# Attention and two mixtures of experts on one core: wide reciprocals, two first pairs taken together, and the decoding of the fourth weight block put behind the last ordered pair

## The chip, the cores and the metric

The kernel runs on one core of one Trainium2 chip. The metric is the device time of one execution in microseconds; the times given are medians of several runs. An engine's name is PE (TensorE), DVE (VectorE), ACT (ScalarE), POOL (GpSimd) or SP (SyncE, which only issues transfers here).

## What is computed

Attention over 4 batches, 12 heads, 448 positions and 64 numbers per head, with queries and keys normalised by their root mean square; then a dense feed-forward layer on the 1792 tokens of 768 numbers; then a layer in which a gate sends each token to one of 8 experts. The reference, cut:

```python
def _attn_ref(q, k, v, g_q, g_k):
    def rmsnorm(x, g):
        rms = np.sqrt(np.mean(x * x, axis=-1, keepdims=True) + 1e-06)
        return x / rms * g
    q_n, k_n = (rmsnorm(q, g_q), rmsnorm(k, g_k))
    scale = 1.0 / np.sqrt(q.shape[-1])
    scores = scale * np.matmul(q_n, k_n.transpose(0, 1, 3, 2))
    scores = scores - np.max(scores, axis=-1, keepdims=True)
    attn = np.exp(scores)
    attn = attn / (np.sum(attn, axis=-1, keepdims=True) + 1e-09)
    return np.matmul(attn, v).astype(np.float32)

def _moe_ref(x, w_in, w_out):          # x 1792x768, w_in 768x2048, w_out 2048x768
    h = x @ w_in
    g = np.maximum(0.01 * h, h)
    return (g @ w_out).astype(np.float32)

def _moe2_ref(x, w_gate, w_output_gate, w1, w2):   # 8 experts, 768 to 1024 to 768
    ...
    for e in range(E):
        mask = e_idx == e
        ...
        h = np.maximum(x[mask] @ w1[e], 0.0)
        ye = h @ w2[e]
        out[mask] = gate_w[mask, None] * eom[mask, e, None] * ye
    return out.astype(np.float32)
```

## The kernel before

**Attention** goes over 24 pairs: a batch and two heads that share the 128 partitions. The 448 positions are cut into 4 chunks (`NC`) of 112 rows (`CP`). For one pair:

- `load` fetches queries and keys (`qk`) and values (`vv`); `square` squares on ACT (`sq`) and sums on DVE (`ms`); `roots` makes the reciprocal roots by nine small DVE steps on all pairs that `together` put side by side; `norm` multiplies (`qn`) on POOL, and for the first pair one half of it on DVE.
- `turn_k` and `turn_q` transpose `qn` on PE (bank `tr`) and split the result in a high and a low part (`kh`, `qh` on ACT, `kl`, `ql` on DVE), of which three products make up one.
- `top` makes the scores of one chunk a first time in a bank `tp`, whose maxima DVE takes (`md`); `row` transposes the four maxima (`tr`, then `mx` on ACT).
- `probs` makes the scores of a chunk with all parts and less the maximum (`sc`, four matmul lines); ACT takes their exp (`p`, for chunk 0 `pr`). `values` multiplies them with `vv` into `av`. POOL adds the four `p` up in `pr`.
- `sums` and `back` bring the sums of the exps, by PE (`tr`, ACT `sp`, then `av`), to DVE, which takes the reciprocal `r`, 112x8. `spread` brings `r` to the layout of `av` (`tr`), `scale` copies that on ACT (`rt`) and multiplies `av` on DVE, and `store` splits the result into `xTh` (ACT) and `xTl` (DVE), the input of the next layer.

The bank `tp` and the bank of `sc` exist once, `tr` twice (`TRB`). So a `top` waits for the `md` of the one before, and `probs` for the exp of the one before.

Pairs 0 to 2 are written out in `begin`, pairs 3 to 22 in `steady` (`prev` is the pair before, `one`, `two` and so on those behind `cur`). There the order of PE, DVE, ACT and POOL is that of the code (`manual_schedule`). The last pair goes by `ORDER`, and a scheduler sets units of the first feed-forward layer in its gaps.

**Weights.** The feed-forward weights lie in memory as 64-bit numbers. `Weights.decode` turns half a block, 128x384 numbers, into 32-bit ones: one transfer into `wd` (one buffer), `mag` on ACT, `top` twice, a compare, `pw` and `raw` on DVE, an add into `raw` on POOL. `RAW` is 3, the number of blocks that can wait in `raw`; `split` turns a block to its high and low part (ACT, POOL). Six halves are decoded within pairs 8 and later (`work(i)`), every second pair one. The halves after these are decoded in `advance`, which the scheduler places; the matmuls of the first layer (`first`, `second`: `mo`, `mp`) take their weights from there.

Of the kernel before, what the change touches and what calls it, by code (L numbers as in the profile page):

```python
# [20 lines left out]
def attention_moe_moe2(  # L21
# [40 lines left out]
    def lo_of(engine, dst, src, hi):  # L62
        engine.tensor_tensor(dst, src, hi.bitcast(F32), ALU.subtract)  # L63
# [91 lines left out]
    class Attention:  # L155
# [30 lines left out]
        def square(self, st):  # L186

            n = 4 * NC
            flat = st["qk"].rearrange("p t h (c d) -> p (t h c) d", d=DH)
            sq = self.early.tile([CP, n, DH], F32, name="sq", bufs=2)  # L190
            for h in (slice(0, n // 2), slice(n // 2, n)) if st is self.first else (slice(0, n),):
                nc.scalar.activation(sq[:, h], flat[:, h], AF.Square, scale=DH ** -0.5)
                nc.vector.tensor_reduce(st["ms"][:, h], sq[:, h], AX.X, ALU.add)
# [68 lines left out]
        def turn_k(self, st, i):  # L262
# [5 lines left out]
            nc.vector.scalar_tensor_tensor(kl, tk, gg, kh.bitcast(F32), ALU.mult, ALU.subtract)  # L268
            st.update(kh=kh, kl=kl)

        def top(self, st, c):

            sc = self.tp()
# [78 lines left out]
        def store(self, st):  # L352
# [3 lines left out]
            lo_of(nc.vector, xl, t, xh)  # L356

        def pieces(self):
# [35 lines left out]
            for op in ORDER:  # L394
                if op == "S":
                    self.sums(sts[n - 2])
                    self.back(sts[n - 2])
                elif op == "C":
# [7 lines left out]
            self.back(last)  # L406
            yield
# [5 lines left out]
        def begin(self, i, sts):  # L413

            cur, one, prev = sts[i], sts[i + 1], sts[i - 1] if i else None
            if i == 0:
                todo = [[("square", 2)], [("roots", 2, 3), ("norm", 2)], [("square", 3)],
                        [("square", 4), ("roots", 3, 5)]]
            elif i == 1:
                todo = [[("norm", 3)], [("square", 5)], [("norm", 4)], []]  # L420
            else:
                todo = [[("square", 6)], [("roots", 5, 7), ("norm", 5)], [("norm", 6)], []]
            for lo, hi in {0: ((2, 3), (3, 5)), 1: ((5, 7),)}.get(i, ()):
                self.together(sts[lo:hi])
            for c in range(NC):
                if c == 3 and prev:
                    self.scale(prev)
                self.probs(cur, c)
                if i == 0 and c == 0:
                    self.turn_k(one, 1)  # L430
                    self.turn_q(one, 1)
                self.top(one, c)
                if c == 2 and prev:
                    self.back(prev)
                if c:
# [5 lines left out]
                elif c == 2 and prev:  # L441
                    self.spread(prev)
# [13 lines left out]
        def steady(self, i, sts):  # L456
# [46 lines left out]
            self.back(prev)  # L503
            self.values(cur, 1)
            self.spread(prev)
# [5 lines left out]
            if at(i + 6):  # L511
                self.square(at(i + 6))
            yield

            self.scale(prev)
            self.probs(cur, 3)
            if two:
                self.top(two, 0)
            self.values(cur, 2)
            self.store(prev)  # L520
            self.row(one)
# [14 lines left out]
    class Weights:  # L536
# [26 lines left out]
        def decode(self, parts=2):  # L563

            n = D // 2
            for _ in range(parts):
# [13 lines left out]
                nc.scalar.activation(mag, hi.bitcast(F32), AF.Abs)  # L580
                nc.vector.tensor_scalar(top, hi, 3, 0x3FFFFFF8, ALU.logical_shift_left, ALU.bitwise_and)
# [530 lines left out]
```

## Time and profile before

| | |
|---|---|
| median of 3 runs | 1232.29 us (1229.84 to 1232.62) |
| profiled execution | 1230.19 us, span of its trace 1228.4 us |
| PE busy | 1158.2 us, 94% of the span |
| DVE busy | 775.5 us, 63% |
| ACT busy | 500.3 us, 41% |
| POOL busy | 456.4 us, 37% |

The shares are averages over parts of the program with different limits; attention ends at some 365 us, and everything that the change touches lies before 420 us. In the trace, a time in square brackets is how long the engine was idle ahead of an instruction, and what it then waited for. PE's records of the same line in a row are put into one row with their count.

### The profile page before, as it was taken

The numbers are of one execution on the slowest core, as the hardware profiler recorded it, in microseconds if no ns is written. First come the engines' busy times: TensorE is split into PE (matmuls) and PEld (weight loads), VectorE is DVE, ScalarE is ACT, GpSimd is POOL, SyncE is SP. The second block draws the span as 40 slices with busy tenths as digits, with TensorE's granted clock in tenths as the row PEclk, the third lists the DMA queues.
The fourth block names the chain that finished last, engine by engine and source line by source line (L and its number), as shares of the span: only waits on it lengthen the run. The fifth ranks groups of instructions, "written<-read, shape, count | busy, mean of one in ns | idle before, by whom it ended". The sixth has DMA issues, their size and how long they took to land.

```text
span 1228.4 us, 19094 instructions
## 1 busy us (share of the span) xinstructions
PE 1158.2 (94%) x6988; PEld 930.8 (76%) x6988; DVE 775.5 (63%) x1326; ACT 500.3 (41%) x791; POOL 456.4 (37%) x301
## 2 busy tenths in 40 slices
PE   4899999989899899999999999999799999999997
PEld 2455555545568788888888889888598988998986
DVE  6777888876627786858585854446745179215446
ACT  2566666655335422222222321132344167225444
POOL 1667767757324331313232220000414047113334
PEclk9999999989899999999999999999699999999999
DMA  5212222111102220202020200343357059413456
GB/s 149 60 47 61 68 80 73 50 29 29 46 13 77 78 77 26 78 26 78 26 78 26 78 26 1 133 118 88 117 199 249 24 197 354 153 47 125 172 201 227
DMA packets 68081, 116.28 MB, mean 95 GB/s; under 512 B 6780, under 2 KB 45948, under 8 KB 67968
## 3 DMA queue, kind: packets, MB, share of 16 engines
q1 hardware_dynamic: 64528, 103.87, 26.6%
q0 software_dynamic: 3120, 11.02, 2.6%
q8 instruction: 57, 0.93, 0.3%
q14 instruction: 56, 0.46, 0.1%
q10 hardware_dynamic: 320, 0.00, 0.0%
HBM read 106.61 MB, written 12.58 MB: 97 GB/s over the span
## 4 chain that ended last, share of the span: by engine, by line
PE 77%; DVE 10%; issue 5%; ACT 3%; DMA 2%; POOL 2%; ACTq 0%; DVEq 0%; POOLq 0%; SPq 0%
PE mo L627 6%; PE mo L628 6%; PE mo L629 6%; PE sc L298 6%; PE av L309 6%; PE mp L646 6%; PE mp L647 5%; PE mp L648 5%; PE ph L990 4%; PE ph L989 3%; PE ph L988 3%; PE py L1006 3%; PE py L1004 3%; PE py L1005 3%; DVE w1l L63 2%
## 5 line engine op out<-in xcount | busy, mean ns | idle before, releaser
L654 DVE TENSOR_TENSOR ysum<-mp,ysum 128x448 f32<-128x448 f32 x168 | 103.8, 621 | 111.1 <-PE mp L648 109.5
L313 POOL TENSOR_TENSOR pr<-pr,p 112x896 f32<-112x896 f32 x72 | 153.2, 2128 | 49.6 <-ACT p L300 35.4
L627 PE MATMUL mo<-xTh,w0h 128*128 128x448 f32 x384 | 142.8, 372 | 13.2 <-DVE g L634 9.4
L646 PE MATMUL mp<-gh,w1h 128*128 128x448 f32 x384 | 144.4, 377 | 1.4 <-ACT ysum L652 0.7
L628 PE MATMUL mo<-xTl,w0h 128*128 128x448 f32 x384 | 141.8, 369 | 0.2 <-DVE xTl L63 0.2
L647 PE MATMUL mp<-gl,w1h 128*128 128x448 f32 x384 | 141.8, 369 | 0.0
L629 PE MATMUL mo<-xTh,w0l 128*128 128x448 f32 x384 | 141.4, 368 | 0.0
L648 PE MATMUL mp<-gh,w1l 128*128 128x448 f32 x384 | 140.4, 368 | 0.0
L588 POOL TENSOR_TENSOR raw<-raw,top 128x384 f32<-128x384 f32 x64 | 65.2, 1020 | 191.1 <-DVE raw L586 166.7
L277 DVE TENSOR_REDUCE md<-tp 112x2 f32<-112x896 f32 x96 | 104.4, 1088 | 17.7 <-PE tp L275 17.4
L1004 PE MATMUL py<-w2h,hT 128*128 128x384 f32 x288 | 99.7, 346 | 0.0
L63 POOL TENSOR_TENSOR w1l<-r,w1h 128x1024 fp32r<-128x1024 f32 x17 | 42.9, 2528 | 149.4 <-ACT w1h L952 75.1
L1006 PE MATMUL py<-w2l,hT 128*128 128x384 f32 x288 | 96.8, 336 | 0.0
L1005 PE MATMUL py<-w2h,hL 128*128 128x384 f32 x288 | 96.5, 335 | 0.0
L63 DVE TENSOR_TENSOR hL<-pt,hT 128x512 fp32r<-128x512 f32 x36 | 24.8, 689 | 106.3 <-ACTq L1014 59.3
L627 PEld LDWEIGHTS mo<-xTh,w0h 128*128 128x128 f32 x384 | 72.5, 189 | 24.1 <-DVE g L634 12.1
L990 PE MATMUL ph<-w1l,xgh 128*128 128x512 f32 x216 | 86.4, 400 | 4.2 <-DVE w1l L63 4.2
L988 PE MATMUL ph<-w1h,xgh 128*128 128x512 f32 x216 | 86.7, 402 | 0.0
L989 PE MATMUL ph<-w1h,xgl 128*128 128x512 f32 x216 | 85.8, 397 | 0.0
L63 POOL TENSOR_TENSOR w1l<-raw,w1h 128x768 fp32r<-128x768 f32 x16 | 31.4, 1984 | 141.7 <-ACT w1h L596 141.7
L646 PEld LDWEIGHTS mp<-gh,w1h 128*128 128x128 f32 x384 | 72.4, 189 | 13.0 <-DVE ysum L654 4.1
L300 ACT ACTIVATE p<-sc 112x896 f32<-112x896 f32 x72 | 66.0, 917 | 39.8 <-PE sc L298 35.6
(199 smaller groups left out, 2499.8 us busy)
## 6 DMA issues: line engine op xcount, KB each, us to landing
r<-in_moe_w_dram SPq DMA_DIRECT2D x27, 1024.0 KB, 5.5
r<-in_moe_w_dram SPq DMA_DIRECT2D x36, 768.0 KB, 7.3
wd<-in_moe_w_in_dram SPq DMA_DIRECT2D x32, 384.0 KB, 3.3
wd<-in_moe_w_out_dram SPq DMA_DIRECT2D x32, 384.0 KB, 3.1
qk<-in_q_dram SPq DMA_DIRECT2D x24, 224.0 KB, 3.0
qk<-in_k_dram SPq DMA_DIRECT2D x24, 224.0 KB, 3.2
vv<-in_v_dram SPq DMA_DIRECT2D x24, 224.0 KB, 2.8
x2d<-xn SPq DMA_DIRECT2D x24, 224.0 KB, 2.9
```

What stands on the lines that cost most here:

```text
L63: engine.tensor_tensor(dst, src, hi.bitcast(F32), ALU.subtract)
L313: nc.gpsimd.tensor_tensor(st["pr"][:CP], st["pr"][:CP], p, ALU.add)
L627: nc.tensor.matmul(ph, wh_[:, c], xh, start=(c == 0), stop=False)
L628: nc.tensor.matmul(ph, wh_[:, c], xl, start=False, stop=False)
L629: nc.tensor.matmul(ph, wl_[:, c], xh, start=False, stop=(c == KD - 1))
L646: nc.tensor.matmul(py, hi[:, sl], gh, start=(j == 0), stop=False)
L647: nc.tensor.matmul(py, hi[:, sl], gl, start=False, stop=False)
L648: nc.tensor.matmul(py, lo[:, sl], gh, start=False, stop=(j == GF - 1))
L990: nc.tensor.matmul(ph[n], xh[:, c], w1l[:, c, s_], start=False, stop=(c == K1 - 1))
L1004: nc.tensor.matmul(py[n], hT[:, c], w2h[:, c, s_], start=(c == 0), stop=False)
L1005: nc.tensor.matmul(py[n], hL[:, c], w2h[:, c, s_], start=False, stop=False)
L1006: nc.tensor.matmul(py[n], hT[:, c], w2l[:, c, s_], start=False, stop=(c == K2 - 1))
```

## The change

Four things. `spread` no longer multiplies each of the eight columns of `r` by the identity, but transposes a copy `wide` (112x512) of `r`, each number 64 times, which ACT makes (`widen`); in `steady` it moves from behind `values(cur, 1)` to behind `row(one)`, and `scale` behind `values(cur, 2)`. At the start, the first two pairs' squares and roots are taken together, both transposes of pair 1 stand among the tops of pair 0, and these tops use the `sc` bank for every second chunk. In `begin`, pair 2 has its roots alone, and pairs 3 and 4 theirs one pair later. And the `mag` and the first `top` of the fourth block (`k == RAW`) are issued after the store seen last (`issue_after`). The diff, cut:

```diff
@@ constants
+    def join_constants():
         nc.vector.scalar_tensor_tensor(gg, gg, ROOT ** -2, gk, ALU.mult, ALU.mult)
@@ norm
-                (nc.vector if t and st is self.first else nc.gpsimd).tensor_tensor(
+                (nc.vector if st is self.first else nc.gpsimd).tensor_tensor(
@@ top
-        def top(self, st, c):
-            sc = self.tp()
+        def top(self, st, c, other=0):
+            sc = self.sc() if other else self.tp()
@@ widen, spread
+        def widen(self, st):
+            wide = self.pool.tile([CP, NC, 2, DH], F32, name="wide", bufs=1)
+            nc.scalar.activation(
+                wide, st["r"].rearrange("p j c -> p c j").unsqueeze(3).to_broadcast([CP, NC, 2, DH]), AF.Copy)
+            st["wide"] = wide
+
         def spread(self, st):
-            tr = st["tr"] = self.tr()
-            for c in range(NC):
-                for j in range(2):
-                    nc.tensor.matmul(
-                        tr[j * DH:(j + 1) * DH, c * CP:(c + 1) * CP],
-                        st["r"][:, j, c:c + 1].to_broadcast([CP, DH]), ident[:CP, :CP], start=True, stop=True)
+            st["tr"] = self.turned_of(st["wide"].rearrange("p c j d -> p c (j d)"))
@@ the start
-                st = sts[0]
-                self.together(sts[:1])
+                st, one = sts[:2]
+                self.together(sts[:2])
                 self.square(st)
-                self.roots(sts[:1])
-                self.norm(st)
+                self.square(one)
+                join_constants()
+                self.roots(sts[:2])
+                self.norm(st, (1, 0))
+                self.norm(one, (1, 0))
                 self.turn_k(st, 0)
                 self.turn_q(st, 0)
-                self.together(sts[1:2])
                 for c in range(NC):
-                    self.top(st, c)
+                    self.top(st, c, c % 2)
                     if c == 1:
-                        self.square(sts[1])
-                self.roots(sts[1:2])
+                        self.turn_k(one, 1, apart=True)
+                        self.turn_q(one, 1, apart=True)
                 self.row(st)
-                self.norm(sts[1])
+                one["klow"]()
+                one["low"]()
...
@@ begin
-                        [("square", 4), ("roots", 3, 5)]]
+                        [("square", 4)]]
             elif i == 1:
-                todo = [[("norm", 3)], [("square", 5)], [("norm", 4)], []]
+                todo = [[("roots", 3, 5), ("norm", 3)], [("square", 5)], [("norm", 4)], []]
...
@@ steady
             self.back(prev)
+            if at(i + 6):
+                self.square(at(i + 6), (0,))
+            self.widen(prev)
             self.values(cur, 1)
-            self.spread(prev)
...
-            self.scale(prev)
             self.probs(cur, 3)
             if two:
                 self.top(two, 0)
+            self.row(one)
+            self.spread(prev)
             self.values(cur, 2)
+            self.scale(prev)
             self.store(prev)
-            self.row(one)
@@ decode
-                nc.scalar.activation(mag, hi.bitcast(F32), AF.Abs)
-                nc.vector.tensor_scalar(top, hi, 3, 0x3FFFFFF8, ALU.logical_shift_left, ALU.bitwise_and)
+                with tc.issue_after(att.stored.ins) if k == RAW else ExitStack():
+                    nc.scalar.activation(mag, hi.bitcast(F32), AF.Abs)
+                with tc.issue_after(att.stored.ins) if k == RAW else ExitStack():
+                    nc.vector.tensor_scalar(top, hi, 3, 0x3FFFFFF8, ALU.logical_shift_left, ALU.bitwise_and)
```

How this moves instructions on three engines follows; line numbers of the changed kernel are its own (L306 is probs, L308 exp, L317 values, L283 top, L285 `md`, L290 row, L254 the transposes of keys, queries and `wide`, L343 `r`, L349 `wide`, L360 scale, L597 to L604 the decoding).

PE in a steady pair, from `back` (`av<-ident,sp`) on, before:

```order
L332 MATMUL av<-ident,sp 112x4 x2
L309 MATMUL av<-p,vv 64x448 x2
L342 MATMUL tr<-ident,r 64x112 x8
L298 MATMUL sc<-qh,kh 112x448 x2
L298 MATMUL sc<-ql,kh 112x448 x2
L298 MATMUL sc<-qh,kl 112x448 x2
L298 MATMUL sc<-mx,mask 112x448 x2
L275 MATMUL tp<-kh,qh 112x448 x2
L309 MATMUL av<-p,vv 64x448 x2
L282 MATMUL tr<-ident,md_137 128x112 x4
L248 MATMUL tr<-ident,qn 128x112 x4
```

The same place in the changed kernel:

```order
L340 MATMUL av<-ident,sp 112x4 x2
L317 MATMUL av<-p,vv 64x448 x2
L306 MATMUL sc<-qh,kh 112x448 x2
L306 MATMUL sc<-ql,kh 112x448 x2
L306 MATMUL sc<-qh,kl 112x448 x2
L306 MATMUL sc<-mx,mask 112x448 x2
L283 MATMUL tp<-kh,qh 112x448 x2
L290 MATMUL tr<-ident,md_139 128x112 x4
L254 MATMUL tr<-ident,wide 128x112 x4
L317 MATMUL av<-p,vv 64x448 x2
L254 MATMUL tr<-ident,qn 128x112 x4
```

Spread moved behind row, which itself moved ahead of the values of that chunk; the keys' transposes now stand alone behind values.

DVE in the pair in which the seventh half, the first of the fourth block, was decoded (L581 to L585), before:

```order
L277 TENSOR_REDUCE md_139<-tp 112x2
L63 TENSOR_TENSOR ql<-tr,qh 128x448
L581 TENSOR_SCALAR top<-wd 128x384
L277 TENSOR_REDUCE md_139<-tp 112x2
L582 SCALAR_TENSOR_TENSOR top<-wd,top 128x384
L335 RECIPROCAL r<-av 112x8
L583 SCALAR_TENSOR_TENSOR top<-mag,top 128x384
L585 TENSOR_SCALAR pw<-top 128x384
L350 TENSOR_TENSOR av<-av,rt 128x448
L277 TENSOR_REDUCE md_137<-tp 112x2
L63 TENSOR_TENSOR xTl_115<-av,xTh_114 128x448
```

In the changed kernel that half stands behind the scale and `xTl` of the last pair but one, with units of the first layer (`g`, `gl`) around it:

```order
L360 TENSOR_TENSOR av<-av,rt 128x448
L652 TENSOR_TENSOR g<-mo,g 128x448
L63 TENSOR_TENSOR xTl_115<-av,xTh_114 128x448
L599 TENSOR_SCALAR top<-wd 128x384
L600 SCALAR_TENSOR_TENSOR top<-wd,top 128x384
L63 TENSOR_TENSOR gl<-g,gh 128x448
L601 SCALAR_TENSOR_TENSOR top<-mag,top 128x384
L603 TENSOR_SCALAR pw<-top 128x384
L604 SCALAR_TENSOR_TENSOR raw<-wd,pw 128x384
L652 TENSOR_TENSOR g<-mo,g 128x448
L599 TENSOR_SCALAR top<-wd 128x384
```

Three more halves follow there, and the last pair's `r` comes behind them.

ACT in the pair in which the seventh half stood, before:

```order
L325 COPY sp<-tr 128x224
L300 ACTIVATE p<-sc 112x896
L580 ACTIVATE mag<-wd 128x384
L348 ACTIVATE rt<-tr 128x448
L300 ACTIVATE p<-sc 112x896
L355 ACTIVATE xTh_114<-av 128x448
L284 ACTIVATE mx<-tr 128x448
L267 ACTIVATE kh<-tr,gg 128x448
```

The same place in the changed kernel:

```order
L333 COPY sp<-tr 128x224
L308 ACTIVATE p<-sc 112x896
L597 ACTIVATE mag<-wd 128x384
L349 ACTIVATE wide<-r 112x512
L308 ACTIVATE p<-sc 112x896
L292 ACTIVATE mx<-tr 128x448
L358 ACTIVATE rt<-tr 128x448
L365 ACTIVATE xTh_114<-av 128x448
L273 ACTIVATE kh<-tr,gg 128x448
```

`mag` of that half stayed in its pair, and `rt` moved behind the last exp and `mx`.

## Rows read from the trace of the kernel before

**Rows 1.** Table of stretches: busy time of each engine, granted clock, DMA share, GB/s.
```profile
100.00:150.00 50.00, 49.95 (x447) 28.28 (x448) 39.25 (x68) 31.93 (x48) 36.04 (x23) 1.00 0.23 66
...
260.00:270.00 10.00, 7.28 (x46) 4.60 (x48) 5.90 (x9) 2.96 (x5) 4.72 (x3) 0.66 0.00 0
...
310.00:320.00 10.00, 9.22 (x54) 4.01 (x54) 7.26 (x11) 2.63 (x4) 3.92 (x2) 0.69 0.21 62
```

**Rows 2.** Chain that ended last, one steady pair: start, us, engine, line.
```profile
92.20 0.90 PE tr L342 x16
...
95.20 0.53 PE tr L282 x4
95.74 0.38 PE tr L248 x4
...
98.23 0.53 PE tr L248 x4
...
103.96 0.90 PE tr L342 x16
```

**Rows 3.** Timeline of the start: start, us, engine, line, instruction.
```profile
13.53 0.71 PE L275 MATMUL tp<-kh,qh 64*112 64x448 f32 x2 [0.63 <-ACT qh L256]
...
28.14 0.57 PE L298 MATMUL sc<-qh,kh 64*112 64x448 f32 x2
```

**Rows 4.** The page's table of transfers: KB each, us to landing.
```profile
qk<-in_k_dram SPq DMA_DIRECT2D x24, 224.0 KB, 3.2
```

**Rows 5.** Timeline of pair 1, where TensorE waits at its end.
```profile
37.61 4.28 POOL L313 TENSOR_TENSOR pr<-pr,p 112x896 f32<-112x896 f32 x2
...
39.85 2.08 DVE L214 TENSOR_SCALAR y<-ms 112x32 int32<-112x32 int32 x1
...
45.69 0.45 PE L275 MATMUL tp<-kh,qh 64*112 64x448 f32 x2 [3.42 <-DVE md L277]
```

**Rows 6.** Waits of TensorE's weight loads, 85 to 250 us: total, times, longest.
```profile
PEld tp L275 <- DVE md L277: 2.2, 5, 0.4
```

**Rows 7.** Timeline of a steady pair with decoding.
```profile
134.18 0.56 DVE L582 SCALAR_TENSOR_TENSOR top<-wd,top 128x384 int32<-128x384 int32 x1
...
136.12 0.56 DVE L586 SCALAR_TENSOR_TENSOR raw<-wd,pw 128x384 f32<-128x384 uint32 x1
...
139.24 0.20 DVE L335 RECIPROCAL r<-av 112x8 f32<-112x8 f32 x1
...
140.58 0.55 ACT L348 ACTIVATE rt<-tr 128x448 f32<-128x448 f32 x1 [0.93 <-PE tr L342]
...
144.25 0.68 DVE L268 SCALAR_TENSOR_TENSOR kl<-tr,gg,kh 128x448 fp32r<-128x448 f32 x1 [0.67 <-ACT kh L267]
```

**Rows 8.** Timeline where the seventh half is decoded.
```profile
261.12 1.42 DVE L582 SCALAR_TENSOR_TENSOR top<-wd,top 128x384 int32<-128x384 int32 x1
...
262.72 1.76 PE L342 MATMUL tr<-ident,r 112*64 112x112 f32 x16 [3.97 <-DVE r L335]
```

**Rows 9.** Waits of TensorE, 250 to 330 us.
```profile
PE tr L342 <- DVE r L335: 5.0, 2, 4.0
PE tp L275 <- DVE md L277: 2.2, 1, 2.2
PE mo L627 <- DVE md L277: 1.9, 1, 1.9
PE sc L298 <- ACT mx L284: 0.7, 1, 0.7
PE sc L298 <- ACT p L300: 0.7, 2, 0.4
```

**Rows 10.** Chain that ended last, 250 to 330 us: one of its longest pieces.
```profile
300.91 3.30 DMA wd<-in_moe_w_out_dram
```

**Rows 11.** Timeline of TensorE behind the last pair and at 415 us.
```profile
365.97 0.47 PE L627 MATMUL mo<-xTh,w0h 128*128 128x448 f32 x1 [1.89 <-ACT xTh L355]
...
415.10 0.69 PE L627 MATMUL mo<-xTh,w0h 128*128 128x448 f32 x1 [4.08 <-DVE g L634]
```

More of the change, by code (lines that the diff above doesn't have):

```diff
@@ L62, in lo_of @@
     def lo_of(engine, dst, src, hi):
-        engine.tensor_tensor(dst, src, hi.bitcast(F32), ALU.subtract)
+        return engine.tensor_tensor(dst, src, hi.bitcast(F32), ALU.subtract)
     cst = ctx.enter_context(tc.tile_pool(name="cst", bufs=1))
@@ L184, in load_v, with square @@
                 st["v"], v[b, 2 * hp:2 * hp + 2].rearrange("h (p c) d -> p h (c d)", c=NC))
-        def square(self, st):
+        def square(self, st, parts=(0, 1)):
             n = 4 * NC
             flat = st["qk"].rearrange("p t h (c d) -> p (t h c) d", d=DH)
-            sq = self.early.tile([CP, n, DH], F32, name="sq", bufs=2)
+            if 0 in parts:
+                st["sq"] = self.early.tile([CP, n, DH], F32, name="sq", bufs=2)
+            sq = st["sq"]
             for h in (slice(0, n // 2), slice(n // 2, n)) if st is self.first else (slice(0, n),):
-                nc.scalar.activation(sq[:, h], flat[:, h], AF.Square, scale=DH ** -0.5)
-                nc.vector.tensor_reduce(st["ms"][:, h], sq[:, h], AX.X, ALU.add)
+                if 0 in parts:
+                    nc.scalar.activation(sq[:, h], flat[:, h], AF.Square, scale=DH ** -0.5)
+                if 1 in parts:
+                    nc.vector.tensor_reduce(st["ms"][:, h], sq[:, h], AX.X, ALU.add)
         def together(self, sts):
@@ L267, in turn_k @@
             nc.scalar.activation(kh, tk, AF.Copy, scale=gg)
-            nc.vector.scalar_tensor_tensor(kl, tk, gg, kh.bitcast(F32), ALU.mult, ALU.subtract)
+            st["klow"] = lambda: nc.vector.scalar_tensor_tensor(kl, tk, gg, kh.bitcast(F32), ALU.mult, ALU.subtract)
+            if not apart:
+                st["klow"]()
             st.update(kh=kh, kl=kl)
-        def top(self, st, c):
-            sc = self.tp()
+        def top(self, st, c, other=0):
+            sc = self.sc() if other else self.tp()
             for j, rows in enumerate(HALVES):
@@ L355, in store @@
             nc.scalar.activation(xh, t, AF.Copy)
-            lo_of(nc.vector, xl, t, xh)
+            self.stored = lo_of(nc.vector, xl, t, xh)
         def pieces(self):
@@ L397, in pieces @@
                     self.back(sts[n - 2])
+                    self.widen(sts[n - 2])
                 elif op == "C":
@@ L406, in pieces @@
             self.back(last)
+            self.widen(last)
             yield
@@ L417, in begin @@
                 todo = [[("square", 2)], [("roots", 2, 3), ("norm", 2)], [("square", 3)],
-                        [("square", 4), ("roots", 3, 5)]]
+                        [("square", 4)]]
             elif i == 1:
-                todo = [[("norm", 3)], [("square", 5)], [("norm", 4)], []]
+                todo = [[("roots", 3, 5), ("norm", 3)], [("square", 5)], [("norm", 4)], []]
             else:
                 todo = [[("square", 6)], [("roots", 5, 7), ("norm", 5)], [("norm", 6)], []]
-            for lo, hi in {0: ((2, 3), (3, 5)), 1: ((5, 7),)}.get(i, ()):
+            for lo, hi in {0: ((3, 5),), 1: ((5, 7),)}.get(i, ()):
                 self.together(sts[lo:hi])
             for c in range(NC):
-                if c == 3 and prev:
-                    self.scale(prev)
                 self.probs(cur, c)
-                if i == 0 and c == 0:
-                    self.turn_k(one, 1)
-                    self.turn_q(one, 1)
                 self.top(one, c)
@@ L434, in begin @@
                     self.back(prev)
+                    self.widen(prev)
+                elif c == 3 and prev:
+                    self.spread(prev)
+                    self.scale(prev)
                 if c:
@@ L440, in begin @@
                     self.sums(prev)
-                elif c == 2 and prev:
-                    self.spread(prev)
                 elif c == 3 and prev:
@@ L503, in steady @@
             self.back(prev)
+            if at(i + 6):
+                self.square(at(i + 6), (0,))
+            self.widen(prev)
             self.values(cur, 1)
-            self.spread(prev)
             if not begun:
@@ L511, in steady @@
             if at(i + 6):
-                self.square(at(i + 6))
+                self.square(at(i + 6), (1,))
             yield
-            self.scale(prev)
             self.probs(cur, 3)
@@ L518, in steady @@
                 self.top(two, 0)
+            self.row(one)
+            self.spread(prev)
             self.values(cur, 2)
+            self.scale(prev)
             self.store(prev)
-            self.row(one)
             if three:
```

3 lines of the change are left out of this document (2 added, 1 removed).

## The prediction

> **What bounds the kernel now.** I read the table of stretches first. In the steady pairs TensorE is busy 49.95 of 50 us at a granted clock of 1.00, while VectorE is busy 39 of 50 and ScalarE 32 [rows 1]: there TensorE alone sets the pace, and only work taken off it, or a wait put into it, counts. At the end of attention the same table has poor stretches, 7.28 of 10 us at clock 0.66 and 9.22 at 0.69. The chain that ended last then shows what a steady pair consists of: TensorE work only, and from one spread (L342) to the next 103.96 − 92.20 = 11.76 us [rows 2]. The timeline of the start shows TensorE held by the row maxima: the first top at 13.53, and still 28.14 before pair 0's second probs [rows 3]; at 45.69 it has waited 3.42 for `md` [rows 5]. The timeline and the waits of the poor stretches show who is late there: a VectorE that stands in decoding of weights, while TensorE waits for `r` (3.97) or `md` [rows 8, 9], and then runs at the lower of its two clocks for some microseconds more.
>
> The profiled execution took 1230.19 us, 2.1 less than the median of the runs; the sum goes by it. A difference under 0.3% (3.7 us) can't be told from none.
>
> **Narrower spread.** Before, a pair spends on transposes: spread 0.90, row 0.53 with keys 0.38 behind it, and queries 0.53 [rows 2]. A group that begins after another kind of matmul costs 0.53, one that stands right behind another group 0.38. After the change spread is four transposes right behind row (0.38), and the keys stand alone after values (0.53): 0.53 + 0.38 + 0.53 + 0.53 = 1.97 against 2.34, −0.37. For the 15 steady pairs 3 to 17 that is −5.6, for the six spreads behind them −2.2; pairs 0 to 2 are in the term for the start.
>
> The new copy `wide` is ScalarE's, 112x512; the nearest row is its 128x448 copy `rt`, 0.55 [rows 7]. It stands between the third and the last exp of a pair, on an engine with 18 of 50 us free. It costs TensorE nothing as long as `r` is early: spread now comes behind another chunk's scores, a top and row as well, some 1.5 us later in the pair, so 0.6 for `wide` fits. What is late instead is the chain behind the spread, `rt`, the scale of `av`, `xTh` and `xTl`: it begins those 1.5 us later too, and `kh`, `kl` and the row maximum of the next tops, which now end 4.4 us after `rt` begins (144.25 + 0.68 − 140.58), queue behind it on ScalarE and VectorE instead of standing clear of it. I laid that order out with the durations of [rows 7]: the exp of the next pair's first probs is 0.4 later relative to TensorE, and the bank for that pair's third top is free 0.1 to 0.2 us before TensorE wants it. In a pair without decoding nothing is lost by this. In a pair with decoding VectorE has about 2.4 us more (five instructions, 0.56 the longest [rows 7]), and is late already: five waits of `tp` for `md`, 2.2 us in all, the longest 0.4 [rows 6]. I take 0.5 more in each of these five, +2.5 (bounds 0, where the later scale falls into VectorE's idle time, and +1.0 in all 15 pairs, +15, where the chain through the scale becomes the period).
>
> **The joined start.** Pair 1's keys are the fourth transfer of queries and keys, and such a one lands 3.2 us after its issue [rows 4], by the order of the issues at about 7.7; then come square, reduce and one chain of roots for both pairs. I get the first top at 15.4, 1.9 later than now. Then the tops alternate between two banks, so that TensorE need not wait for each `md`; pair 1's transposes are done beside them, and pair 0's second probs begin at 25.7 instead of 28.14 (−2.4). The next gain is the stall before 45.69: a VectorE instruction of the roots, 2.08 us long, with a slow one ahead of it, holds `kl` and `md`, and TensorE waits 3.42 [rows 5] and then runs slowly for 4 us. The roots now stand behind that pair's first `md`. I get pair 2's third top 7.4 earlier than now; some 0.5 for `wide` goes off again in the first spreads, and a first spread that is narrower gives as much back. The term is −8 (bounds −4, where the stall only moves to the next `md`, and −10).
>
> What made that instruction slow is a matter of ports. The 2.08 was for a step on 112x32 numbers while a POOL add ran [rows 5]; L582, 0.56 alone, took 1.42 beside one [rows 7, 8]. The Trainium skill (SBUF — State Buffer, "Who interferes with whom") says that a VectorE operation in a two-port mode and a GpSimd operation exclude each other, whoever issues first, for the whole instruction; the trace agrees. By that rule the roots in their new place are slow again if a POOL add runs then, and the start would give −4.
>
> **The fourth weight block.** The half that is decoded around 259 us goes behind the last ordered `xTl` on VectorE. Now its `top` and L582 stand with an `md` ahead of `r`; TensorE idles 3.97 [rows 8] and then runs at half clock to about 268. The halves behind it do the same around 302 to 316. From 250 to 330 the waits of TensorE that name another engine are 5.0 + 2.2 + 1.9 + 0.7 + 0.7 = 10.5 [rows 9]; the 1.9 of L627 is behind an ordered pair and stays, 8.6 go. What the low clock costs in the two stretches is the busy time by what is missing of the clock, 7.28 × 0.34 + 9.22 × 0.31 = 5.4 [rows 1]. Together −14 (bounds −9, where the splitting of the first weights alone keeps VectorE, ScalarE and POOL late around 300, and −16 with the 1.9).
>
> Against this stand two costs. The half's `mag` on ScalarE does not move: in the new order it stands directly ahead of `wide` of one ordered pair and waits for its weights. Its transfer takes 3.3 [rows 10] from when the half before it has left the buffer (in a pair like it 136.68, the end of `raw`), and `mag` about 0.55; `r` ends at 139.44 there, 2.8 after [rows 7]. So `wide` starts 1.1 late, with 0.3 of slack: +0.8 (0 to 4). And halves 7 to 10 now run one after the other, each a transfer of 3.3 [rows 10] and 2.4 of VectorE, all behind `xTl` of the last pair but one. Some of these instructions stand ahead of the last `r`, on which the last scale and the first matmuls of its batch wait, by 1.89 already [rows 11]. I get that `r` 2.7 late (0 to 5); with `wide` 0.3 and 0.5 for what is queued behind, +3.5 (0 to 8). The weights themselves are needed later: the tenth half ends where it ended.
>
> **Sum.** −8 − 5.6 − 2.2 + 2.5 − 14 + 0.8 + 3.5 = −23.0, so 1230.2 − 23.0 = 1207.2 in a profiled execution. Runs lay 0.4 below to 2.4 above that one; I say 1208.
>
> **The rivals.**
> *The bound passes to the scale chain.* If spread, `rt`, `av`, `xTh`, `kh`, `kl`, `md` become the period of each steady pair, the 5.6 is lost, and 0 to +3 comes in the place of the 2.5. For it: margins of 0.1 to 0.2 us in my layout. Against it: VectorE's 11 idle us of 50 and ScalarE's 18 [rows 1]. Time 1208 + 5.6 − 1 = 1213. Chance 0.2.
> *The tail eats it.* If the four halves meet POOL adds as L582 did in [rows 8] (each instruction 1 us longer, five or more of them ahead of the last `r`), the tail costs 5 to 8 more, some of it as low clock: 1215. For it: that row. Against it: POOL is partly idle at the end. Chance 0.12.
> *The change doesn't do what it says:* `mag`, still in its old place on ScalarE, stalls `wide` by as long as `r` was stalled, 3.97, and the clock falls once more (2.5): +6.5 in the place of the 0.8, 1214. For it: the order. Against it: one instruction, not a chain of four, is ahead. Chance 0.06.
> *Slower.* Waits at `tp` long enough to lower the granted clock in every decoding pair. In this trace the clock fell after waits of 3.42, 3.97 and 4.08, and not after 1.89 [rows 5, 8, 11]; from some 3 us a pair it decides. Five pairs at 3 of idle time and 2.5 for slow matmuls are +27.5 in the place of +2.5, 1233; with the same at `wide` in the pair of `mag`, 1238. Against it: the longest such wait now is 0.4 [rows 6]. Chance 0.05.
> *More gain.* The 4.08 before 415.10 [rows 11] waits for the activation of a first-MoE unit whose VectorE queue is reordered here; if it goes, with the slow matmuls behind it, 1202. Chance 0.1.
>
> **How the numbers follow.** My own case has 0.47, with a range of 1201 to 1215; the others are as above, and 1208 is the likeliest. The range 1196 to 1222: the start at −10, the junction at −16, nothing for decoding pairs, `mag` and tail are 10.8 less, 1197; the start at −4, the junction at −9 and the tail at +8 are 13.5 more, 1221. It leaves out the slower case and about as much of the ends. The time is the same as before (1228.6 to 1236) if almost all of the bad bounds come together or the slower rival stays small: 0.06. Slower 0.05, faster 0.89.
>
> **What would show it.** Right: no gap of TensorE over 1 us from the second probs to about 320; stretches between 250 and 320 above 9.5 of 10 at clock 1.00; spread right behind row with 0.38; a steady period of 11.4; the last `r` behind decoding on VectorE. Wrong: TensorE under 49 of 50 in steady stretches, with waits for `md` or `wide`; a `kl` or `md` held by roots around 42; waits of 4 us or more around the last `r`; a clock under 1.00 in the ordered pairs.

## The result and the profile after

The changed kernel took 1209.74 us, median of 4 runs (1208.93 to 1211.22), against 1232.39 for the kernel before; the ratio is 0.9822 with a 95% interval of 0.9805 to 0.9839, so it is 1.8% faster. The profiled execution has a span of 1207.2 us, 21.2 shorter than before.

Its table of stretches (busy time of PE, PEld, DVE, ACT and POOL, granted clock, DMA share, GB/s) answers to [rows 1]:

```profile
100.00:150.00 50.00, 49.87 (x398) 27.64 (x400) 40.31 (x69) 35.28 (x55) 35.81 (x22) 1.00 0.23 70
...
260.00:270.00 10.00, 10.00 (x82) 5.36 (x82) 6.42 (x9) 6.18 (x11) 6.87 (x5) 1.00 0.10 25
...
310.00:320.00 10.00, 10.00 (x57) 6.91 (x56) 7.05 (x10) 3.71 (x7) 3.43 (x3) 1.00 0.01 2
...
330.00:340.00 10.00, 3.13 (x18) 2.60 (x16) 4.82 (x11) 2.00 (x4) 1.73 (x2) 0.77 0.13 40
340.00:350.00 10.00, 6.79 (x19) 5.33 (x19) 7.01 (x11) 4.36 (x8) 5.26 (x4) 0.55 0.35 95
```

The two poor stretches of [rows 1] are full and at clock 1.00. In their place a new pair of them stands at 330 to 350, at the end of attention. The waits of TensorE there (total, times, longest; 330 to 420 us) name the cause:

```profile
PE tr L254 <- ACT wide L349: 6.9, 1, 6.9
PE mo L645 <- DVE g L652: 4.2, 1, 4.2
PE mo L645 <- ACT xTh L365: 1.9, 1, 1.9
```

The second is the 4.08 of [rows 11] and has not gone; the third is the 1.89 of [rows 11]. The first is new.

The chain that ended last, in a steady pair (answers to [rows 2]):

```profile
109.00 0.53 PE tr L290 x4
109.53 0.38 PE tr L254 x4
109.92 0.90 PE av L317 x4
110.82 0.53 PE tr L254 x4
```

Row, spread right behind it with 0.38, values, keys with 0.53: TensorE alone, as before, with 1.97 of transposes counting the queries' 0.53. The starts of the sums (L329) of two pairs in a row, from the timeline, give the period, 11.40 against 11.76:

```profile
104.61 0.59 PE L329 MATMUL tr<-pr,ones_mat 113*32 113x112 f32 x16
...
116.01 0.59 PE L329 MATMUL tr<-pr,ones_mat 113*32 113x112 f32 x16
```

The start of that row is a good mark for the rest too, since each of the 24 pairs has it once. The table shows where each kernel stands against the one before, by the difference of these starts (us; each is the start in the kernel's timeline less that in the timeline of before; the last two columns are the first matmul of the first layer behind the last store, at 365.97 before, and the span). Starts of profiled executions differ by up to 0.9 (the third line keeps +0.9 from the first pair to the eighteenth).

| kernel | pair 2 | pair 17 | pair 20 | pair 22 | pair 23 | behind the last store | span |
|---|---|---|---|---|---|---|---|
| changed | −7.1 | −12.0 | −19.5 | −34.0 | −33.3 | −24.1 | −21.2 |
| wide spread alone | −0.7 | −5.5 | −6.9 | −14.3 | −14.2 | −10.9 | −7.7 |
| order of the fourth block alone | +0.9 | +0.9 | −5.8 | −15.1 | −11.3 | −8.5 | −4.4 |
| joined start alone | −6.5 | −6.5 | −7.5 | −5.9 | −5.9 | −5.9 | −3.0 |
| changed, fourth block as before | −6.8 | −11.7 | −13.3 | −20.7 | −20.6 | −17.3 | −16.1 |
| changed, last r ahead of the tenth half | −6.8 | −11.6 | −19.2 | −33.7 | −33.0 | −29.2 | −23.5 |

By the first line, 7 come at the start, 5 in the steady pairs, 21 around the decoding near 260 and 300 us; 9 go at the last pair, and 3 behind it. Before the sums of pair 23 the changed kernel has issued 104 matmuls of the first layer, the kernel before 117; 13 at 0.2 are 2.6 of the 21 and of the 9, which only moved. (The first matmul behind the last store is the 124th of that layer in each kernel of the table.)

### The profile page after: what moved, and what is told of

Its sections match the earlier page's. It is cut to its first block, busy times and chain, and to the rows that moved or that the text cites. A ratio compares the mean times of both kernels' runs of the same rounds, so it can differ in the third digit from the quotient of the medians.

```text
span 1207.2 us, 18558 instructions
## 1 busy us (share of the span) xinstructions
PE 1142.3 (95%) x6700; PEld 919.5 (76%) x6700; DVE 770.2 (64%) x1318; ACT 510.2 (42%) x815; POOL 454.0 (38%) x300
## 4 chain that ended last, share of the span: by engine, by line
PE 71%; DVE 15%; ACT 4%; issue 4%; DMA 3%; POOL 2%; ACTq 0%; DVEq 0%; SPq 0%; POOLq 0%
PE mo L645 6%; PE mo L646 6%; PE mo L647 6%; PE sc L306 5%; PE mp L664 5%; PE mp L665 5%; PE mp L666 5%; PE av L317 5%; PE ph L1008 4%; PE ph L1007 3%; PE ph L1006 3%; PE py L1024 3%; PE py L1022 3%; PE py L1023 3%; DVE w1l L63 2%
## 5 line engine op out<-in xcount | busy, mean ns | idle before, releaser
L321 POOL TENSOR_TENSOR pr<-pr,p 112x896 f32<-112x896 f32 x72 | 151.4, 2103 | 33.9 <-ACT p L308 20.7
L645 PE MATMUL mo<-xTh,w0h 128*128 128x448 f32 x384 | 143.4, 374 | 11.4 <-DVE g L652 9.5
L285 DVE TENSOR_REDUCE md<-tp 112x2 f32<-112x896 f32 x94 | 102.2, 1088 | 23.1 <-PE tp L283 22.7
L645 PEld LDWEIGHTS mo<-xTh,w0h 128*128 128x128 f32 x384 | 72.5, 189 | 24.1 <-DVE g L652 12.9
L308 ACT ACTIVATE p<-sc 112x896 f32<-112x896 f32 x72 | 66.0, 916 | 33.6 <-PE sc L306 32.1
```

Of the source, the lines that this page charges most:

```text
L321: nc.gpsimd.tensor_tensor(st["pr"][:CP], st["pr"][:CP], p, ALU.add)
L645: nc.tensor.matmul(ph, wh_[:, c], xh, start=(c == 0), stop=False)
```

## The experiments

**The three parts, each alone.** First the spread (`widen`, the transposes, their places, in `begin` too), on the kernel before:

```diff
-                    nc.tensor.matmul(tr[...], st["r"][:, j, c:c + 1].to_broadcast([CP, DH]), ident[:CP, :CP], ...)
+            st["tr"] = self.turned_of(st["wide"].rearrange("p c j d -> p c (j d)"))
```

> The kernel before with the wide reciprocals and the moved spread, row and scale alone. By parts that add up: 21 spreads (pairs 3 to 23) at -0.37 are -7.8, the period of a steady pair without decoding 11.40 instead of 11.77, about 1224.5 us. Rival, the chain behind the later scale holds the pairs: period 11.8 or more, 1230 to 1236. Rival, the parts need one another (the spread gains only where decoding is gone from the ordered pairs): the junction at 260 and 300 us becomes worse by 2 to 5, about 1228.

Measured: 1222.07 us, ratio 0.9918 (0.9902 to 0.9935). From pair 2 to pair 17 it gains 4.8, or 0.32 a pair; the chain behind the scale holds nothing up. And the parts don't need one another: with the decoding still in the ordered pairs it gains 8.7 more from pair 17 to pair 23, where six narrow spreads account for 2.2 and 15 matmuls of the first layer that moved behind pair 23 for 3.0; the rest is idle time of TensorE, 10.5 before and 7.4 here.

> The kernel before with the joined start and the later roots of pairs 3 and 4 alone (spread by eight matmuls at its old place, decoding as before). By parts that add up: the sums of pair 2 come 7 us earlier, the rest is shifted by as much, about 1225. Rival, the gain is eaten again in the first spreads, since r comes late for a spread that stands right behind values: 3 to 4 us less, about 1229.

```diff
-                self.together(sts[:1])
+                self.together(sts[:2])
...
-                        [("square", 4), ("roots", 3, 5)]]
+                        [("square", 4)]]
```

Measured: 1227.67 us, ratio 0.9967 (0.9955 to 0.9979), between the two times expected. The 6.5 of pair 2 hold to pair 17 and are 3 at the end of the span. Nothing is eaten in the first spreads; the loss is later, around the decoding and behind attention.

> The kernel before with the decoding of the fourth block behind the last ordered pair alone. By parts that add up: about -20 in the ordered pairs 18 to 22 and +12 at the last pair's r and behind it, so -8 to -9, about 1224. Rival, the tail's cost belongs to the copy of r and the later scale, not to the decoding that stands ahead of r: tail +4 or less, -15 and more, about 1216. Rival, the gate gives nothing net: within 3 us of before.

```diff
+                with tc.issue_after(att.stored.ins) if k == RAW else ExitStack():
                     nc.vector.tensor_scalar(top, hi, 3, 0x3FFFFFF8, ALU.logical_shift_left, ALU.bitwise_and)
```

Measured: 1226.88 us, ratio 0.9965 (0.9951 to 0.9979). It gains 16.0 up to pair 22 and loses 6.6 again up to the first matmul behind the last store. So the loss at the end belongs to the decoding ahead of the last pair's steps, not to `wide`. Here `r` stands ahead of the tenth half, and TensorE waits only 0.79 for it; but the last scale stands behind that half's first two instructions, which wait for their weights:

```profile
355.18 0.36 DVE L583 TENSOR_SCALAR top<-wd 128x384 int32<-128x384 int32 x1 [3.33 <-DMA wd<-in_moe_w_in_dram]
...
357.44 0.74 PE L629 MATMUL mo<-xTh,w0h 128*128 128x448 f32 x1 [4.55 <-ACT xTh L355]
```

By spans the three are 7.7 + 4.4 + 3.0 = 15.1 of 21.2; up to pair 23 they are −31.4 of −33.3, so they add up there, and it is in what each gives back later that they don't.

**The changed kernel without the order of the fourth block.**

> The changed kernel with the decoding of the fourth block where it was before (no order behind a store). By parts that add up: start -7 and spreads -7.8 stay, about 1217; the wait of some 4 us for r (now for its copy) near pair 18 is back, and the wait of 6.9 at the last pair is gone. Rival, the decoding behind the ordered pairs costs at the end what it gives before: 1208 to 1211.

```diff
-                with tc.issue_after(att.stored.ins) if k == RAW else ExitStack():
-                    nc.scalar.activation(mag, hi.bitcast(F32), AF.Abs)
+                nc.scalar.activation(mag, hi.bitcast(F32), AF.Abs)
```

Measured: 1214.07 us, ratio 0.9856 (0.9840 to 0.9873), 4.3 slower than the changed kernel and 17 faster than before: between the two times expected. The wait at the last spread is gone, as expected (0.96), but near pair 18 no wait of some 4 is back. There the new place of spread has parted the wait of [rows 8] in two shorter ones:

```profile
249.57 1.43 DVE L598 SCALAR_TENSOR_TENSOR top<-wd,top 128x384 int32<-128x384 int32 x1
249.70 0.45 PE L283 MATMUL tp<-kh,qh 64*112 64x448 f32 x2 [1.50 <-DVE md L285]
...
251.84 1.01 PE L254 MATMUL tr<-ident,wide 112*128 112x112 f32 x4 [1.15 <-ACT wide L349]
```

The same VectorE work in the same pair now costs waits of 1.50 and 1.15 instead of 3.97, since spread stands some 1.7 us later in the pair. The granted clock falls nevertheless (0.66 from 250 to 260 us), so this pair gains little by the place: it takes 17.81 us from mark to mark, where it was 18.67 before and is 11.95 with the order.

**The last r ahead of the tenth half.** `advance` may ask for nine halves while attention runs, and for all behind it:

```diff
+            self.limit = 9
...
-                if len(self.raw) < min(k + RAW, len(self.order)):
-                    self.decode()
+                if self.halves < min(2 * min(k + RAW, len(self.order)), self.limit):
+                    self.decode(1)
                     continue
+                if self.halves < 2 * k + 2:
+                    return
...
+    wts.limit = 2 * len(wts.order)
     sA.close()
```

> The changed kernel with only nine halves of weights asked for while attention runs; the tenth and later ones are asked for behind the last pair's store, so that on VectorE the last r stands ahead of the tenth half instead of behind four of its five instructions. If the tail's loss is that r: the wait of 6.9 at the last spread falls to about 1 to 1.5, the low clock behind it (2.7) goes, and 2 come back later because decoding is then nearer to its users: 1202 to 1204 us. Rival, the weights themselves are late, and the time is given back in the first layer: 1207 to 1211.

Measured: 1206.41 us, ratio 0.9796 (0.9780 to 0.9812), 3.3 less than the changed kernel; the fastest of the study together with the run "together" below. Timeline of the changed kernel at the last spread:

```profile
330.61 0.36 DVE L599 TENSOR_SCALAR top<-wd 128x384 int32<-128x384 int32 x1 [2.82 <-DMA wd<-in_moe_w_in_dram]
...
331.70 0.47 PE L340 MATMUL av<-ident,sp 128*112 128x4 f32 x4
...
336.58 0.36 DVE L599 TENSOR_SCALAR top<-wd 128x384 int32<-128x384 int32 x1 [3.37 <-DMA wd<-in_moe_w_in_dram]
...
338.12 0.20 DVE L343 RECIPROCAL r<-av 112x8 f32<-112x8 f32 x1
...
339.03 1.01 PE L254 MATMUL tr<-ident,wide 112*128 112x112 f32 x4 [6.87 <-ACT wide L349]
...
341.92 0.74 PE L645 MATMUL mo<-xTh,w0h 128*128 128x448 f32 x1 [1.88 <-ACT xTh L365]
```

and with r ahead:

```profile
332.93 0.56 DVE L605 SCALAR_TENSOR_TENSOR raw<-wd,pw 128x384 f32<-128x384 uint32 x1
333.40 0.20 DVE L343 RECIPROCAL r<-av 112x8 f32<-112x8 f32 x1
...
334.32 0.60 PE L254 MATMUL tr<-ident,wide 112*128 112x112 f32 x4 [1.86 <-ACT wide L349]
...
336.80 0.74 PE L648 MATMUL mo<-xTh,w0h 128*128 128x448 f32 x1 [1.88 <-ACT xTh L365]
```

VectorE sits through the 3.37 us in which the tenth half's weights come in, with `r` behind it and its input (L340, 331.70) long there. In the trace three of that half's five instructions stand ahead of `r`, not four. Without them, 5.0 of the 6.87 go. Of the 5.1 that this kernel is ahead behind the last store, 2.3 are left in the span, so the rival had a part of it: TensorE's waits for `ysum`, the sum over the layer's second matmuls, come to 3.9 us from 330 to 450 us, where the changed kernel has 1.5. That the later decoding makes them is likely and not shown.

**The place of the spread.**

> The changed kernel with the transposed spread in its old place in the steady pairs, right behind the values of chunk 1 (row behind values of chunk 2, scale ahead of the last probs, as before); wide is kept. If the place is needed to hide wide: TensorE waits about 0.6 for wide in each steady pair, the period is 11.9 to 12.1 instead of 11.4, about 1220. Rival, the place matters little and the narrower spread alone gives the gain (wide hidden by values): period 11.4 to 11.5, 1209 to 1212.

```diff
             self.back(prev)
+            if at(i + 6):
+                self.square(at(i + 6), (0,))
+            self.widen(prev)
             self.values(cur, 1)
             self.spread(prev)
```

Measured: 1236.17 us, ratio 1.0042 (1.0025 to 1.0059), slower than the kernel before. The period is 12.4 instead of 11.4, worse than expected; some 3 us more of its profiled execution are the granted clock's, which fell in pair 1 (see the last section). That kernel's chain goes through ScalarE's square as well, which stood ahead of `wide`; so one more run put `wide` ahead of the square.

> As the run with the transposed spread in its old place, but with wide ahead of the square on ScalarE: there the square (1.05) stood between the exp and wide and was part of what held the spread. If wide's own time is enough to undo the gain in the old place: TensorE waits 0.5 to 0.7 per steady pair instead of 0.85, the period is 11.9 to 12.0 (before 11.77), 1219 to 1225 us. Rival, the square was the whole reason: the period is 11.4 to 11.5, 1210 to 1212.

Measured: 1226.70 us, ratio 0.9966 (0.9956 to 0.9976), with a period of 12.11, both a little above what was expected; from pair 2 to pair 17 it loses 5.0 against the kernel before. The waits of TensorE from 85 to 240 us, in the first and in the second of these kernels:

```profile
PE tr L254 <- ACT wide L349: 11.1, 13, 1.2
```

```profile
PE tr L254 <- ACT wide L349: 8.3, 13, 0.6
```

and the chain of the second:

```profile
108.35 1.09 DVE md L285
109.44 0.12 DVE r L343
...
109.65 0.64 ACT wide L349
...
110.33 0.60 PE tr L254 x4
```

In its old place the spread had `r` just in time, and `wide` comes on top with its whole 0.64: that is more than the 0.37 that four transposes save. The place behind row hides `wide`: in the changed kernel TensorE has no wait for it from 85 to 330 us.

**Eight matmuls in the new place.**

> The changed kernel with the eight matmuls of r by the identity in place of wide and four transposes, in the new place behind row. It parts the width from the place. If width alone gives the steady gain and the place the gain around the decoding: the steady period is 11.77 (0.37 more than 11.40), the sums of pair 17 come 6 later than in the changed kernel, and what pairs 18 to 23 gain over the kernel before stays but for 0.37 each; about 1217. Rival, the place gives nothing by itself and only lets wide be late: 1217 too in the steady part, but waits for r of 3 or more near 260 come back, 1221 or more. Rival, eight matmuls behind row cost less than 0.9 (as transposes do behind row): period under 11.6, 1213.

```diff
         def spread(self, st):
-            st["tr"] = self.turned_of(st["wide"].rearrange("p c j d -> p c (j d)"))
+            tr = st["tr"] = self.tr()
+            for c in range(NC):
+                for j in range(2):
+                    nc.tensor.matmul(
+                        tr[j * DH:(j + 1) * DH, c * CP:(c + 1) * CP],
+                        st["r"][:, j, c:c + 1].to_broadcast([CP, DH]), ident[:CP, :CP], start=True, stop=True)
```

Measured: 1214.79 us, ratio 0.9860 (0.9845 to 0.9875). The chain of a steady pair:

```profile
100.31 0.53 PE tr L290 x4
100.84 0.92 PE tr L353 x16
```

Behind row the eight matmuls still cost 0.92; the period is 11.77, and pair 17 comes 7.9 later than in the changed kernel. Of this 2.6 are there by pair 2 and are not the eight matmuls': the granted clock fell in pair 1 here (see the last section). No wait for `r` comes back near 260, so the second rival is out. So in the steady pairs the place earns nothing by itself, and the width earns nothing without the place.

**The roots of pairs 3 and 4.**

> The changed kernel with the roots of pairs 3 and 4 where they were, at the end of pair 0, ahead of kl, ql and md. If that chain made the stall of 3.4 there: it is back (nine steps on 112x32, one of them slowed by a POOL add), the sums of pair 2 come 4 to 6 us later than in the changed kernel, about 1214. Rival, the joined start has already moved POOL's adds away, the roots take 2 us without a lock, and the stall is under 1: 1210 to 1211.

```diff
-                        [("square", 4)]]
+                        [("square", 4), ("roots", 3, 5)]]
```

Measured: 1213.84 us, ratio 0.9856 (0.9835 to 0.9877), and pair 2 comes 4.4 later than in the changed kernel. Timeline:

```profile
34.05 6.49 POOL L321 TENSOR_TENSOR pr<-pr,p 112x896 f32<-112x896 f32 x3
...
38.61 1.97 DVE L222 TENSOR_TENSOR a<-y 112x32 f32<-112x32 f32 x1
...
44.12 0.46 PE L283 MATMUL tp<-kh,qh 64*112 64x448 f32 x2 [3.19 <-DVE md L285]
```

The stall of [rows 5] is back, with another step of the roots slowed until POOL's adds end at 40.54. In the changed kernel the same chain begins at 40.09, as POOL's adds end, and no step is held for long: L220, the slow one of [rows 5], takes 0.18.

```profile
40.41 0.18 DVE L220 TENSOR_SCALAR y<-ms 112x32 int32<-112x32 int32 x1
```

**mag, and all together.**

> The changed kernel with mag of the fourth block ordered behind an instruction of ScalarE (xTh of the same store) instead of one of VectorE. If mag ahead of wide is what makes one pair 0.57 longer than the others without decoding (11.95 against 11.40): that pair becomes 11.4, and the time falls by 0.5, too little for the time to show. Rival, the transfer itself or the missing half on VectorE is the reason: the pair stays at 11.9.

```diff
+            self.kept = nc.scalar.activation(xh, t, AF.Copy)
...
-                with tc.issue_after(att.stored.ins) if k == RAW else ExitStack():
+                with tc.issue_after(att.kept.ins) if k == RAW else ExitStack():
                     nc.scalar.activation(mag, hi.bitcast(F32), AF.Abs)
```

Measured: 1210.13 us, a single run. The pair in question takes 11.79 instead of 11.95, as long as the other pairs with a half in them. But in the runs with `r` ahead and with the roots in their old place, where `mag` still stands ahead of `wide`, it takes 11.84 and 11.83; so `mag` there costs 0.04 to 0.16. The expectation had overlooked that this pair, too, still has a half to finish.

> The changed kernel with nine halves asked for during attention (r ahead of the tenth half), mag of the fourth block behind ScalarE's store, and the first pair's queries normalised on POOL again, its keys on VectorE. The first gave 3.3 before, mag is worth 0.16 by the trace, and the queries on POOL may bring the first top from 16.7 to about 16.1, since two products on VectorE beside a POOL product took 2.14: 1205 to 1206. Rival, pair 1's products on POOL are then late by 1.5 and its transposes hold the row of pair 0: 1207 or more.

```diff
-                (nc.vector if st is self.first else nc.gpsimd).tensor_tensor(
+                (nc.vector if t and st is self.first else nc.gpsimd).tensor_tensor(
```

Measured: 1205.90 us (1203.31 to 1207.36), ratio 0.9784 (0.9770 to 0.9798); not to be told from the run with r ahead alone. The first top starts at 16.52 instead of 16.66, and pair 1 comes 0.2 earlier than in the changed kernel: the queries' place gives little. Pair 2 comes 1.4 later, by the clock alone (see the last section).

## Why the prediction was right

It said 1208 and 1196 to 1222, faster; 1209.74 was measured. The mechanisms of the gains held, but that the sum came so near is partly luck. From mark to mark of the profiled execution, with the 2.6 that only moved taken out, the start gave −7.1 (forecast −8), the steady pairs to pair 17 −4.9 (−3.1), the fourth block with its six spreads and `mag` −18.7 (−15.4), and the end of attention with all behind it cost 9.5 (3.5). The last two lie outside the bounds given for their terms and nearly cancel; together it is −21.2, and −23.0 was forecast.

- **Narrower spread**, −0.37 a pair: shown, 11.76 to 11.40. The five pairs with decoding were to lose 0.5 each; they take 11.77 to 11.81, 0.4 more than the others, where before it was 0.3. That is 0.5 in all, not 2.5. The first rival, the chain through the scale as the period, did not come in any run with the spread in its new place; with the spread in its old place a chain through `md`, `r` and `wide` did hold the pairs, as the term on `wide` reasoned.
- **Joined start**, −8: it was −7.1 up to the sums of pair 2, and −6.5 alone. The run with the roots in their old place shows that 4.4 of it is the stall of [rows 5]. The rest was put too high: the first top starts at 16.66, not 15.4, and pair 0's second probs at 26.70, not 25.7, so that they are late by no more than the first top is. Of these 1.3 us the keys of pair 1 make 0.8: ScalarE squares them from 8.47 on, as they land, and not from 7.7 on. The 3.2 of [rows 4] is a median over 24 transfers; this one landed 4.1 after its issue, and 4.8 in the kernel before. The other 0.5 was not taken apart. The row of pair 0 also waits 2.50, in the end for `kl` of pair 1 to leave a bank of `tr`, which was not in the working; but from the first top to the second probs 10.0 pass, and 10.3 were forecast.

```profile
8.47 1.06 ACT L197 ACTIVATE sq<-qk 112x1024 f32<-112x1024 f32 x1 [2.29 <-DMA qk<-in_k_dram]
...
16.66 0.72 PE L283 MATMUL tp<-kh,qh 64*112 64x448 f32 x2 [0.63 <-ACT qh L262]
...
22.95 0.98 PE L290 MATMUL tr<-ident,md 112*128 112x112 f32 x4 [2.50 <-DVE kl L274]
...
26.70 0.71 PE L306 MATMUL sc<-qh,kh 64*112 64x448 f32 x2 [0.64 <-ACT pr L308]
```

- **The fourth block**, −14 with 0.8 for `mag`: from pair 17 to pair 23 the changed kernel gains 21.3; less 2.6 for the moved matmuls and 2.2 for six spreads that is 16.5. The waits of [rows 9] are gone but for one of 0.3, the 1.9 that was to stay among them. That is 1.6 more than forecast, and the 0.8 for `mag` hardly came; the last 1.0 is not explained (the term for the low clock, worked out again, is 5.3 and not 5.4). The order and the narrower spread in its new place share the gain: without the order 8.9 of the 21.3 remain. In the pair of the seventh half nearly all is the order's, as the run without it shows.
- **The end of attention**, +3.5: mis-sized, and the step that failed is the r "2.7 late". It is late by 5.9: its input is there at 332.17, and it starts at 338.12, behind the first instructions of the tenth half, for which VectorE has sat through that half's transfer. The wait is 6.87 against 0.30 in the same place before; waits of 4 us or more around the last `r` were among the prediction's own signs of being wrong. The transfers took 3.2 to 3.4, as forecast. What was in no term of the sum is that POOL's adds slow two instructions on the way: L600 of the seventh half takes 2.54 and L601 of the eighth 2.47, each 0.56 when no add runs, 3.9 more in all. Each half's transfer is issued only when the half before has left the buffer (319.13 behind 319.06, 327.31 behind 327.25), so this goes on to `r`; without it `r` would be some 2.0 late, by an estimate from these numbers. By this working the 3.2 over the forecast are the rival "the tail eats it", in size and in mechanism, with two instructions longer by 1.9 to 2.0 in place of five by 1. No run takes the slow instructions away, so this share is worked out and not shown. What is shown is that the place of `r` decides how much of it all is paid: the run with `r` ahead has the same two (2.53 and 2.48), and its wait is 5.0 shorter.

  Behind the wait the granted clock is low (0.55 from 340 to 350 us), and the first layer takes 7.87 from its first matmul behind the store to the one at 349.79, where the same stretch took 5.97 before: another 1.9, 0.7 of it in a longer wait for `xTl`.

```profile
314.45 2.13 POOL L321 TENSOR_TENSOR pr<-pr,p 112x896 f32<-112x896 f32 x1 [4.00 <-ACT p L308]
314.45 2.54 DVE L600 SCALAR_TENSOR_TENSOR top<-wd,top 128x384 int32<-128x384 int32 x1
...
323.76 2.08 POOL L321 TENSOR_TENSOR pr<-pr,p 112x896 f32<-112x896 f32 x1 [3.62 <-ACT p L308]
323.79 2.47 DVE L601 SCALAR_TENSOR_TENSOR top<-mag,top 128x384 f32<-128x384 f32 x1
```

- **`mag`** does not move, as the order showed, and costs 0.04 to 0.16 (0.8 forecast, the rival 4 and more).
- **More gain** did not come: the 4.08 before 415.10 is 4.17 before 392.94.

Of the excess at the end, the run with r ahead gives back 5.1 behind the last store and 3.3 in the time. Behind that store the changed kernel, the spread alone and the joined start alone lose some 3 us of their gain by spans, the order alone 4. In the changed kernel 1.9 of its 2.9 are those up to 349.79; most of the rest is one wait some 90 us later, 1.06 where it was 0.33 before:

```profile
436.39 0.44 PE L664 MATMUL mp<-gh,w1h 128*128 128x448 f32 x1 [1.06 <-DVE ysum L672]
```

Why this `ysum` is late stays open.

## What to carry to other kernels

Here VectorE waited at the head of its queue, so an order between two instructions moved the whole chain behind it. What has to be read is what then stands ahead of the last step that others wait for: one half with its transfer of 3.4 us in front of a reciprocal cost 5. A chain of transfers and instructions, each waiting for the one before, also hands on every delay on its way: two instructions slowed by POOL's adds made it 3.9 longer. A cheaper form of a step that needs a copy first is worth its saving only in a place where the copy's time is covered; move the step first, then make it narrow. And take each term from one mark to the next (here one row that every pair has): a sum can come out right while two of its parts are wrong in opposite directions, as here.

## What was not expected of the hardware

- The granted clock fell after two waits of 1.50 and 1.15 within 2.5 us of one another (0.66 from 250 to 260 us in the changed kernel without the order). The prediction took a single wait of some 3 to be what decides, and read [rows 11] wrongly for it: behind the 1.89 there, which follows one of 0.30, matmuls of the kernel before take 0.57 from 367.68 on, so the clock fell there too. It did not fall behind the 1.9 of L627 in [rows 9], ahead of which TensorE had no wait of 0.3 or more for some 9 us (1.00 from 320 to 330 us).
- The same waits can lower the clock in one kernel and not in another. In pair 1 TensorE waits 0.37, 0.55 and 1.19 in the changed kernel and 0.38, 0.55 and 1.19 in the run with the spread in its old place. The clock stays at 1.00 in the first and falls in the second (0.50 from 67 to 71 us), where it is 18.17 us from the mark of pair 1 to that of pair 2, and not 15.12:

```profile
65.49 0.46 PE L283 MATMUL tp<-kh,qh 64*112 64x448 f32 x2 [1.19 <-DVE md L285]
65.87 0.97 PE L317 MATMUL av<-p,vv 112*64 112x448 f32 x4
```

```profile
65.22 0.71 PE L283 MATMUL tp<-kh,qh 64*112 64x448 f32 x2 [1.19 <-DVE md L285]
65.87 1.76 PE L317 MATMUL av<-p,vv 112*64 112x448 f32 x4
```

  It also fell there in the run with eight matmuls in the new place (18.06, with waits of 0.71 and 1.19) and in the run with all together (16.70, with the waits of the first), and in no other run. So up to 3 us between two profiled executions can be this alone.
- A pair's eight matmuls of 64x112 cost 0.90 to 0.92 whether they stand behind another kind of matmul or behind transposes, while a group of four transposes costs 0.53 in the first place and 0.38 in the second.
- The step of the roots that a POOL add slows is not a fixed one: L214 in the kernel before (2.08), its third step L222 in the run with the roots in their old place (1.97). It is the one that VectorE starts next after an add has begun (38.61 after 38.40 in the second); this was seen twice and not varied on purpose. The Trainium skill (SBUF — State Buffer, "Who interferes with whom") says that a VectorE instruction with two inputs in SBUF contends with a POOL instruction that reads SBUF, and calls it an exclusive lock. The trace agrees for L222, which has two such inputs: it ends at 40.58, POOL's adds at 40.54.
